# A three-part transformer kernel on one core: first batch in a new written order, second batch's keys on VectorE, third batch's keys behind the last output product, values in parts of 256 and 320 tokens

## The chip, the core and the metric

The kernel runs on one core of a Trainium2 chip. The metric is device time in microseconds of one execution, the median of several runs. Before the change it is 943.38 us (three runs, 940.66 to 943.66).

The engines are TensorE (matrix products, PE in the rows; a transposition is a product with the identity), VectorE (DVE), ScalarE (ACT), GpSimd (POOL) and SyncE (SP), which issues the DMAs. Each takes its instructions in the order in which they are written; semaphores hold them until what they read has been written and what they write over has been read.

## What is computed

Three blocks on 8 batches of 576 tokens: attention against keys and values pooled by 8 (8 heads of 64), a gated MLP with a spatial product, and a mixture of four attention experts. The change touches the first two only.

```python
k_p = k.reshape(B, H, Sp, pool, D).mean(axis=3); v_p = v.reshape(...).mean(axis=3)   # 576 -> 72 keys
attn = softmax(scale * q @ k_p.T)
x = (attn @ v_p) -> [B, S, 512]
h = gelu(x @ w_in)                       # w_in 512 x 1024
u, v = h[..., :512], h[..., 512:]
v_n = (v - mean) / sqrt(var + 1e-6) * g_ln
v_s = w_sg @ v_n + b_sg                  # over the tokens, 576 x 576
x = x + (u * v_s) @ w_out
out = experts(x)                         # q, k, v of 4 experts, causal softmax, top 2 gating
```

## The kernel before

Phase A does attention and the gated MLP batch by batch and stores `x` to DRAM; phase B does the experts for all batches. From the second batch on, most products are made of three float32r matmuls, of high and low halves (`wih`, `wil`, `xh`, `xl`); a `split` copies the high half on ScalarE and subtracts on VectorE. The first batch computes in plain float32, since it has to make these halves of the weights while it runs.

A batch of phase A has these stages. The keys are pooled into the block matrix `kbd` (`pool_k`, L206: per half an addition of 576 columns, one of 288, two of 144). Scores of five chunks of tokens (128, the last 64) go to PSUM (`score`, L274), then maximum, exponential (`probs`, or eight activations per chunk inside `score` for the chunks listed in `AXT`), sum, reciprocal and product `P` (`finish`, L307). `trans` (L324) transposes `P` by five TensorE transpositions and ScalarE copies it to `pth`; from the second batch on VectorE also makes the low half `ptl`. The values are pooled (`pool_v`), and the products with the values give `x` (`av`, in the first batch `av_first`, L373, in two halves of 288 tokens). The projection to `v` comes first (`vfirst`, L445, 32 matmuls in the trace, then `vpart` for the last chunk), then that to `u` (`upart`, L499), each with a gelu on ScalarE. Layer norm (`norm`, `scaled`) is done by VectorE, with the power on GpSimd and the high half on ScalarE. `spatial` (L518) makes four products, each multiplied with `u` by VectorE (L533), copied high by ScalarE (L538) and low by VectorE (L540, the steps `L` in the first batch). `outp` (L546) makes four output products from these; VectorE adds `x` (L560) and takes the low half (L562).

Within a batch, the next batch's scores, finishes and transpositions lie between these products.

The middle batches are written out in `middle`. The first batch's order is a string, `SEQ`: one token is one step (a letter, then its number), and all its instructions on PE, DVE, ACT and POOL keep this order. In it `a`, `b`, `d`, `h`, `g` are loads, `p` pools the first batch's keys, `s`, `x`, `f`, `t` are score, exponential, finish and transposition of a chunk, `y` pools values, `z` is a half of `av_first`. `G` and `W` turn one eighth of `w_in` from 64-bit to 32-bit (`W4` to `W7` are those of `v`, one for each 128 rows; `W0` to `W3` those of `u`), `D` splits it, `Y` is a step of `vfirst`, `V` and `U` the other projections, `n` and `N` the norm, `S` a part of `w_sg`, `o`, `E`, `O`, `Z` the four parts of `w_out`, `P` a spatial product. `K`, `k`, `Q`, `C`, `X`, `F`, `R`, `v` load and pool the second batch's keys (`k`), load `q`, score, exponentiate, finish its chunks, load and pool its values. Tables beside it choose PSUM buffers (`ST`, `TRT`, `AT`, `VT`), the engine that pools keys (`KE`: D for VectorE, P for GpSimd) and the number of dummy transpositions of the identity ahead of a step, which only keep TensorE busy (`idle`, L269: `WS` ahead of a score, `WT` ahead of a transposition, `WV` ahead of a half of `av_first`).

The third batch's keys are pooled by GpSimd, their first half at the start of `middle(1)` (L655); as GpSimd's queue has nothing else then, it starts when the keys have landed.

Of the kernel before, what the change touches and what calls it, by code (L numbers as in the profile page):

```python
# [12 lines left out]
AF = mybir.ActivationFunctionType  # L13
# [3 lines left out]
B, H, S, D = 8, 8, 576, 64  # L17
# [2 lines left out]
NT = 5  # L20
TINY64 = 2.0 ** -30 * 1.265625
NV = ['DD', 'DD', 'DD', 'DD', 'DD']
TRT = ("mm", "tr", "sc", "mm", "mm")
PV = [None, None, 0]
ST = ('mm','mm','sc','tr','mm')
PK = [(0,), (1,), ()]
WOF = 4
XW = 4 * (640 + S)
AXT = {(0, 0), (0, 2), (0, 4), (1, 2), (1, 3), (1, 4)}
FD = {(0,2), (0,3), (0,4), (0, 0), (0, 1), (1, 0), (1, 1), (1, 2), (1, 3), (1, 4)}  # L30
ORD = (mybir.EngineType.PE, mybir.EngineType.DVE, mybir.EngineType.Activation, mybir.EngineType.Pool)
AT = (("tr", "sc"), ("mm", "mm"))
WV = (8,0)
VT = ("sc", "tr")
CT = ("sc", "tr", "sc", "tr", "sc")
XA = (0, 1, 2, 3)
WS = (0, 0, 0, 0, 0)
WT = (14,26,8,0,8)
VE = ('PPP', 'PPP')
KE = ('DD','PP')  # L40
SE = 'DDDD'
SEQ = ("a0 a1 b0 b1 b2 b3 b4 d0 d1 d2 c h2 h3 g h0 h1 p0 p1 s0 x0 s1 x1 s2 x2 f0 s3 x3 s4 t0 f1 x4 t1 "
# [4 lines left out]
TOK = [(i * 128, min(128, S - i * 128)) for i in range(NT)]  # L47


class PhaseA:  # L50


    def __init__(self, ctx, tc, w, ins, x2d):
# [6 lines left out]
        self.EX, self.WO, self.MV = {}, {}, {}  # L60
        self.PT, self.VN, self.QT, self.KV, self.RAW, self.STG = {}, {}, {}, {}, {}, {}


    def load_k(self, b, parts=(0, 1)):
        nc, w = self.nc, self.w
# [307 lines left out]
    def av_first(self, h):  # L373

        nc, mm = self.nc, self.nc.tensor.matmul
        pt, (v, vl) = self.PT[0][0], self.KV[0]
        s = slice(h * HS, h * HS + HS)
        if h == 0:
            xu = self.XU[0] = self.w.tile([128, 2368 * 2], F32, tag="xu", name="xu")
            for p in range(NP):  # L380
                self.X32[0, p] = xu[:, p * S:p * S + S].rearrange("p (a n) -> p a n", a=2)
        x = self.XU[0][:, :NP * S].rearrange("p (c n) -> p c n", c=NP)
        ps = [self.ps.tile([128, 2, 512], F32, tag=t, name="av", bufs=2 if t == "mm" else 1) for t in AT[h]]
        self.idle(ps[0][:, 0, :128], WV[h])
        for p in range(NP):
            r = slice(32 * p, 32 * p + 32)
            mm(ps[p // 2][:, p % 2, :HS], vl[r].rearrange("p a b -> p (a b)"), pt[r, 4, s], start=True, stop=False, skip_group_check=True)
        for p in range(NP):
            mm(ps[p // 2][:, p % 2, :HS], v[:, p], pt[:, p, s], start=False, stop=True, skip_group_check=True)
            if p % 2:  # L390
                nc.scalar.activation(x[:, p - 1:p + 1, s], ps[p // 2][:, :, :HS], AF.Copy)

    def put_x(self, b, p, ps):
        nc, w = self.nc, self.w
# [123 lines left out]
    def spatial(self, b, d):  # L518
        nc, w = self.nc, self.w
        vh, vl = self.VN[b]  # L520
        ps = self.ps.tile([128, 2, 512], F32, tag="mm", name="sp", bufs=2)
        c = slice(d * 128, d * 128 + 128)
        for h in range(2):
            s = slice(h * HS, h * HS + HS)
            o = ps[:, h, :HS]
            for k in range(4):
                nc.tensor.matmul(o, vh[:, k, c], self.ws[0][:, k, s], start=k == 0, stop=False)  # L527
                nc.tensor.matmul(o, vl[:, k, c], self.ws[0][:, k, s], start=False, stop=False)  # L528
                nc.tensor.matmul(o, vh[:, k, c], self.ws[1][:, k, s], start=False, stop=False)  # L529
            nc.tensor.matmul(o, vh[:, 4, c], self.ws[0][:, 4, s], start=False, stop=False)  # L530
            nc.tensor.matmul(o, self.vn2[:, c], self.ws[1][:, 4, s], start=False, stop=True)
        u = self.U.pop((b, d))
        nc.vector.tensor_mul(u, ps[:, :, :HS], u)  # L533
        if d == 0:
            self.GG[b] = w.tile([128, 2368 * 2], F32R, tag="xg", name="g")
        part = lambda i: self.GG[b][:, i * S:i * S + S]
        gh, gl = (part(i).rearrange("p (a n) -> p a n", a=2) for i in (d, 4 + d))
        nc.scalar.activation(gh, u, AF.Copy)  # L538
        self.G[b, d] = (part(d), part(4 + d))
        low = lambda: (nc.gpsimd if b and d < 3 else nc.vector).tensor_sub(gl, u, gh.bitcast(F32))  # L540
        if b:
            low()
        else:
            self.low[d] = low
# [51 lines left out]
    def first(self):  # L596
# [32 lines left out]
        if B > 1:  # L629
            steps.update({  # L630
                "K": lambda i: load_k1(), "k": lambda i: pool_k1(), "Q": lambda i: self.load_q(1), "R": lambda i: load_v1(),
                "v": lambda i: behind(lambda: self.pool_v(1), self.rs), "M": lambda i: self.parts_v(), "C": lambda i: self.score(1, i),
                "X": lambda i: self.probs(1, i),
                "F": lambda i: self.finish(1, i)})
        keep, last = ORD, {}
# [14 lines left out]
    def middle(self, b):  # L650
# [1 line left out]
        n = b + 1  # L652
        more = n < B
        if more:
            self.pool_k(n, PK[0])  # L655
        for t in (0, 2, 4):
            self.vpart(b, t)
            if more and t == 0:
# [478 lines left out]
```

## Time and profile before

| | us |
|---|---|
| median of three runs | 943.38 |
| profiled execution | 941.85 |
| its span, first to last instruction | 940.1 |
| TensorE busy | 913.8 (97%) |
| VectorE busy | 676.8 (72%) |
| ScalarE busy | 513.7 (55%) |
| GpSimd busy | 415.5 (44%) |

The profile's page shows TensorE above 90% in nearly all of its 40 slices; the first two and a few at the start have less. So the stages are read one by one. A row of the timeline gives start, busy time, engine, line, operation, what it writes and reads, and the count; in brackets the idle time just before it and who ended it. Matmuls overlap by their pipeline, so the distance of two starts tells more than the busy time.

### The profile page before, as it was taken

The page shows a single profiled execution, that of the slowest core. Times are in us where ns is not written, and L with a number is a line of the kernel's source. Part 1 is how long each engine was busy: PE and PEld are TensorE (multiplying, and loading weights), DVE is VectorE, ACT ScalarE, POOL GpSimd, SP SyncE. Part 2 cuts the span into 40 slices and gives each one's busy share as a digit, 9 for nine tenths or more (in the row PEclk, how much of TensorE's full clock was granted, in tenths as well). Part 3 has the DMA queues.
Part 4 walks back from the last instruction along what each step waited for, and adds up shares of the span by engine and source line. Part 5 has one row for each costly group of instructions (what it writes and reads, how often), then busy time and mean ns, then how long its engine had stood idle before and what let it go on. Part 6 is the DMA issues. An engine that isn't in the chain of part 4 may idle for free.

```text
span 940.1 us, 18379 instructions
## 1 busy us (share of the span) xinstructions
PE 913.8 (97%) x6496; PEld 858.0 (91%) x6496; DVE 676.8 (72%) x1844; ACT 513.7 (55%) x1280; POOL 415.5 (44%) x590
## 2 busy tenths in 40 slices
PE   6998999999999999999999999899999999999997
PEld 5577999999899899899999999899999999999987
DVE  6899577577586676676675435797978787878785
ACT  4755343343443443434343425677778786777686
POOL 4336268377475683693683440122223232322221
PEclk9999999999999999999999999999999999999999
DMA  9724204214123124024034023435344342525121
GB/s 322 268 68 157 103 12 137 109 42 142 76 85 124 62 74 155 30 74 174 12 116 157 18 97 89 133 86 162 100 138 122 109 141 90 169 64 167 51 63 77
DMA packets 51644, 102.86 MB, mean 109 GB/s; under 512 B 10592, under 2 KB 16736, under 8 KB 50656
## 3 DMA queue, kind: packets, MB, share of 16 engines
q1 hardware_dynamic: 51408, 101.68, 33.2%
q8 instruction: 52, 0.85, 0.4%
q14 instruction: 40, 0.33, 0.1%
q10 hardware_dynamic: 144, 0.00, 0.0%
HBM read 59.72 MB, written 28.31 MB: 94 GB/s over the span
## 4 chain that ended last, share of the span: by engine, by line
PE 79%; DVE 12%; ACT 4%; issue 2%; DMA 1%; SPq 1%; POOL 0%; ACTq 0%; DVEq 0%; POOLq 0%
PE av L1026 4%; PE op L555 4%; PE op L556 4%; PE sc L283 4%; PE op L557 4%; PE up L511 3%; PE sp L529 3%; PE up L513 3%; PE sp L527 3%; PE sp L528 3%; PE up L512 3%; PE vp L442 3%; PE vp L440 3%; PE vp L441 3%; PE t L1006 3%; PE pj L833 3%
## 5 line engine op out<-in xcount | busy, mean ns | idle before, releaser
L980 POOL TENSOR_SCALAR pr<-pr,sm,gw 128x128 f32<-128x128 f32 (+3 forms) x119 | 72.1, 608 | 210.8 <-DVE sm L976 137.5
L964 ACT ACTIVATE pr<-s,sm 128x256 f32<-128x256 f32 (+4 forms) x160 | 83.1, 520 | 41.4 <-DVE sm L961 19.6
L555 PE MATMUL op<-g,woh 128*128 128x288 f32 x256 | 77.8, 308 | 2.0 <-DVE xu L533 1.4
L527 PE MATMUL sp<-wsh,vnh 128*128 128x288 f32 x256 | 78.0, 305 | 0.5 <-DVE xu L533 0.5
L556 PE MATMUL op<-g,woh 128*128 128x288 f32 x256 | 76.7, 300 | 0.8 <-DVE g L540 0.8
L833 PE MATMUL pj<-xbh,wqh 128*128 128x288 f32 x256 | 75.7, 296 | 0.0
L834 PE MATMUL pj<-xbl,wqh 128*128 128x288 f32 x256 | 75.6, 295 | 0.0
L529 PE MATMUL sp<-wsl,vnh 128*128 128x288 f32 x256 | 75.4, 295 | 0.0
L835 PE MATMUL pj<-xbh,wql 128*128 128x288 f32 x256 | 75.4, 295 | 0.0
L528 PE MATMUL sp<-wsh,vnl 128*128 128x288 f32 x256 | 75.4, 294 | 0.0
L557 PE MATMUL op<-g,wol 128*128 128x288 f32 x256 | 75.0, 298 | 0.0
L511 PE MATMUL up<-x,wih 128*128 128x288 f32 x224 | 67.3, 300 | 0.0
L513 PE MATMUL up<-x,wil 128*128 128x288 f32 x224 | 66.2, 295 | 0.0
L512 PE MATMUL up<-x,wih 128*128 128x288 f32 x224 | 65.7, 293 | 0.0
L961 DVE CUSTOM_DVE_ANT_0 s<-s,mk 128x512 f32<-128x512 f32 (+3 forms) x128 | 62.3, 487 | 2.9 <-PE t L1006 2.6
L1011 DVE TENSOR_TENSOR pbl<-t,pbh 128x512 fp32r<-128x512 f32 (+3 forms) x128 | 60.5, 484 | 3.3 <-ACT pbh L1010 1.9
L562 POOL TENSOR_TENSOR x2l<-x2l,x2h 128x576 fp32r<-128x576 f32 x8 | 11.4, 1427 | 111.3 <-ACT x2h L561 111.3
L1006 PE MATMUL t<-ident,pr 128*128 128x128 f32 x320 | 56.4, 278 | 3.3 <-POOL pr L980 3.1
L1026 PE MATMUL av<-pbh,vt 128*128 128x320 f32 (+4 forms) x224 | 56.1, 280 | 2.7 <-ACT pbh L1010 2.7
L283 PE MATMUL sc<-kbd,qt 128*128 128x144 f32 (+1 forms) x320 | 48.0, 297 | 7.7 <-DMA qt<-q_in 7.3
L492 ACT ACTIVATE vnh<-vg,rs 128x512 fp32r<-128x512 f32 (+1 forms) x40 | 27.2, 717 | 51.2 <-POOL rs L474 40.8
L337 ACT ACTIVATE pth<-tr 128x640 fp32r<-128x640 f32 (+3 forms) x40 | 26.0, 653 | 53.1 <-PE tr L336 43.5
(259 smaller groups left out, 3305.7 us busy)
## 6 DMA issues: line engine op xcount, KB each, us to landing
kraw<-k_in SPq DMA_DIRECT2D x16, 576.0 KB, 3.8
x<-x2h SPq DMA_DIRECT2D x32, 288.0 KB, 2.1
x<-x2l SPq DMA_DIRECT2D x32, 288.0 KB, 2.1
xbl<-x SPq DMA_DIRECT2D x32, 288.0 KB, 4.0
xbh<-x SPq DMA_DIRECT2D x32, 288.0 KB, 4.0
kd<-scr SPq DMA_DIRECT2D x64, 144.0 KB, 2.5
out<-o SPq DMA_DIRECT2D x32, 288.0 KB, 3.6
vraw<-v_in SPq DMA_DIRECT2D x16, 512.0 KB, 4.2
```

Of the source, the lines that this page charges most:

```text
L283: nc.tensor.matmul(ps[:m, p // 2, (p % 2) * 144:(p % 2) * 144 + 144], qt[:, p, o:o + m], kbd[:, p, :], start=p % 2 == 0, stop=True, skip_g ...
L511: nc.tensor.matmul(o, self.wi[0][:, kc, c], xh, start=kc == 0, stop=False)
L512: nc.tensor.matmul(o, self.wi[0][:, kc, c], xl, start=False, stop=False)
L513: self.upmm = nc.tensor.matmul(o, self.wi[1][:, kc, c], xh, start=False, stop=kc == 3).ins
L527: nc.tensor.matmul(o, vh[:, k, c], self.ws[0][:, k, s], start=k == 0, stop=False)
L528: nc.tensor.matmul(o, vl[:, k, c], self.ws[0][:, k, s], start=False, stop=False)
L529: nc.tensor.matmul(o, vh[:, k, c], self.ws[1][:, k, s], start=False, stop=False)
L555: nc.tensor.matmul(o, self.wo[0][:, k, c], gh[:, s], start=k == 0, stop=False)
L556: nc.tensor.matmul(o, self.wo[0][:, k, c], gl[:, s], start=False, stop=False)
L557: self.opmm = nc.tensor.matmul(o, self.wo[1][:, k, c], gh[:, s], start=False, stop=k == 3).ins
L833: nc.tensor.matmul(ps, self.wq[0][:, kc, c], xh[:, s], start=kc == 0, stop=False)
L1026: nc.tensor.matmul(ps[:, s - lo:], vt[:, j, 2 * p + e].rearrange("p a d -> p (a d)"), t[:, e, j * PTS + s:j * PTS + up], start=j == 0 and ...
```

## The change

The new order of the first batch is a new string, with new tables of buffers and of dummy transpositions. The second batch's keys go to VectorE (`KE`). In `av_first` the two halves become 256 and 320 tokens (`AZ`). The first half of the third batch's keys waits for the last output product of the first batch (`KL`). A step `v` with another number than 0 could be held back too, but the string has only `v`, which stays as it was. Cut to its core (line numbers below 65 are the same in both; from there the changed kernel's are 13 to 17 higher):

```diff
-TRT = ("mm", "tr", "sc", "mm", "mm")
+TRT = ('mm', 'tr', 'mm', 'mm', 'mm')
-ST = ('mm','mm','sc','tr','mm')
+ST = ('mm', 'tr', 'sc', 'tr', 'mm')
+AZ = ((0, 256), (256, S))
-WV = (8,0)
-VT = ("sc", "tr")
+WV = (0, 6)
+VT = ('tr', 'sc')
-WS = (0, 0, 0, 0, 0)
-WT = (14,26,8,0,8)
+WS = (6, 0, 0, 12, 9)
+WT = (5, 11, 0, 0, 0)
-KE = ('DD','PP')
+KE = ('DD','DD')
+KL = 1
-SEQ = ("a0 a1 b0 b1 b2 b3 b4 d0 d1 d2 c h2 h3 g h0 h1 p0 p1 s0 x0 s1 x1 s2 x2 f0 s3 x3 s4 t0 f1 x4 t1 "
+SEQ = ("a0 a1 b0 b1 b2 b3 b4 d0 d1 d2 c h2 h3 g h0 h1 p0 p1 s0 s1 x0 x1 s2 G5 f0 x2 y0 s3 s4 t0 x4 f1 "
...
+    def behind(self, step, ins, engine):
+        traced = self.nc.cur_bb.bb.instructions
+        n = len(traced)
+        step()
+        for i in traced[n:]:
+            if i.engine == engine:
+                self.tc.add_manual_dep(i, ins.name, mybir.DependencyInfo(mybir.DependencyClass.Sync, mybir.DependencyReason.DATA),
+                                       reason="begun behind it")
+                return
...
-        s = slice(h * HS, h * HS + HS)
+        s = slice(*(AZ[h]))
+        m = s.stop - s.start
...
         if more:
-            self.pool_k(n, PK[0])
+            if b == 1 and KL:
+                self.behind(lambda: self.pool_k(n, PK[0]), self.opmm, mybir.EngineType.Pool)
+            else:
+                self.pool_k(n, PK[0])
```

In the lists that follow `P` is a chunk's probabilities, `tr` and `pth` their transposition in PSUM and in SBUF, `st` the maxima and sums, `sc` scores, `av` the products with the values `v` and `vl`, `w` the 32-bit `w_in` (made from `st` and `g`), `vp` the projection to `v`, `sp` a spatial product, `xu` the array of `x` and `u`, `g` the gated values, `op` an output product.

TensorE, from the second transposition to the projection, before (after its first five transpositions):

```order
L272 MATMUL tr<-ident 128x128 x26
L336 MATMUL tr<-ident,P 128x128 x5
L272 MATMUL tr<-ident 128x128 x8
L336 MATMUL tr<-ident,P 128x128 x5
L272 MATMUL av<-ident 128x128 x8
L387 MATMUL av<-pth,vl_280 128x288 x4
L389 MATMUL av<-pth,v_99 128x288 x4
L336 MATMUL tr<-ident,P 128x128 x5
L272 MATMUL tr<-ident 128x128 x8
L336 MATMUL tr<-ident,P 128x64 x5
L387 MATMUL av<-pth,vl_280 128x288 x4
L389 MATMUL av<-pth,v_99 128x288 x4
```

The same place now:

```order
L285 MATMUL tr<-ident 128x128 x11
L349 MATMUL tr<-ident,P 128x128 x10
L401 MATMUL av<-pth,vl_284 128x256 x4
L403 MATMUL av<-pth,v_99 128x256 x4
L349 MATMUL tr<-ident,P 128x64 x5
L349 MATMUL tr<-ident,P 128x128 x5
L285 MATMUL av<-ident 128x128 x6
L401 MATMUL av<-pth,vl_284 128x320 x4
L403 MATMUL av<-pth,v_99 128x320 x4
```

The dummies (L272, now L285) between the real steps became fewer, the last full chunk and the half one changed places, and the value products have 256 and 320 columns.

VectorE, from the third chunk's `P` of the second batch to the first output product's addition, before:

```order
L316 TENSOR_TENSOR P<-e,st 128x512
L319 TENSOR_TENSOR P<-e,st 128x4x16 x2
L540 TENSOR_TENSOR g<-xu,g 128x576
L312 TENSOR_SCALAR st<-st 64x8
L313 RECIPROCAL st<-st 64x8
L316 TENSOR_TENSOR P<-e,st 64x512
L319 TENSOR_TENSOR P<-e,st 64x4x16 x2
L533 TENSOR_TENSOR xu<-sp,xu 128x576
L340 TENSOR_TENSOR ptl<-tr,pth 128x4x128
L540 TENSOR_TENSOR g<-xu,g 128x576
L341 SCALAR_TENSOR_TENSOR ptl<-pth,cm,tr 128x128
L560 TENSOR_TENSOR op<-op,xu 128x2x288
```

Now, from the low half of the first gated product:

```order
L554 TENSOR_TENSOR g<-xu,g 128x576
L547 TENSOR_TENSOR xu<-sp,xu 128x576
L554 TENSOR_TENSOR g<-xu,g 128x576
L547 TENSOR_TENSOR xu<-sp,xu 128x576
L554 TENSOR_TENSOR g<-xu,g 128x576 x2
L301 TENSOR_REDUCE st<-sc 64x8
L353 TENSOR_TENSOR ptl<-tr,pth 128x4x128
L304 TENSOR_SCALAR st<-st 64x8
L325 TENSOR_SCALAR st<-st 128x8
L354 SCALAR_TENSOR_TENSOR ptl<-pth,cm,tr 128x128
L326 RECIPROCAL st<-st 128x8
```

The multiplications (L533, now L547) and low halves (L540, now L554) stand together ahead of the last three finishes, which come after them with the last score block (L301); the first output product's addition (L574) follows the first of those finishes.

VectorE, from the last splits of `w_in` (`wil`) and `w_sg` (`wsl`) to the first normalisation (`bs`), before:

```order
L155 TENSOR_TENSOR wil<-w_73,wih 128x512
L198 TENSOR_TENSOR wsl<-st_459,wsh 128x576
L155 TENSOR_TENSOR wil<-w_73,wih 128x512
L203 SCALAR_TENSOR_TENSOR wsl<-h_470,cm,st_468 128x576
L155 TENSOR_TENSOR wil<-w_73,wih 128x4x128 x4
L470 BN_STATS bs<-vg 128x6 x2
```

The same place now, up to the first half of the second batch's keys (`kraw`, `kbd`):

```order
L216 SCALAR_TENSOR_TENSOR wsl<-h_436,cm,st_434 128x576
L168 TENSOR_TENSOR wil<-w_73,wih 128x512
L211 TENSOR_TENSOR wsl<-st_443,wsh 128x576
L211 TENSOR_TENSOR wsl<-st_447,wsh 128x576
L224 TENSOR_TENSOR kraw<-kraw 128x576
L225 TENSOR_TENSOR kraw<-kraw 128x288
L228 TENSOR_TENSOR kbd<-kraw 64x2x72 x2
```

The second half of the keys follows with the same three rows, and then `BN_STATS`. Before, these six rows were GpSimd's.

## Rows read from the trace of the kernel before

**Rows 1.** Busy time by stretch: PE, PEld, DVE, ACT, POOL (instructions), granted clock, DMA.

```profile
0.00:105.00 105.00, 92.56 (x514) 73.16 (x515) 85.38 (x162) 58.90 (x167) 42.50 (x66) 0.98 0.54 194
105.00:171.00 66.00, 66.00 (x459) 61.65 (x459) 44.50 (x75) 26.02 (x38) 42.57 (x58) 1.00 0.25 88
```

**Rows 2.** Timeline of TensorE, second transposition to projection; columns as told above.

```profile
18.68 3.03 PE L272 MATMUL tr<-ident 128*128 128x128 f32 x26 [1.22 <-DVE e L296]
...
23.51 1.04 PE L272 MATMUL av<-ident 128*128 128x128 f32 x8
24.56 0.77 PE L387 MATMUL av<-pth,vl 32*128 32x288 f32 x8
...
27.30 0.71 PE L336 MATMUL tr<-ident,P 128*128 128x128 f32 x5
...
32.61 13.90 PE L455 MATMUL vp<-w,xu 128*128 128x512 f32 x32
```

**Rows 3.** Timeline of TensorE, first spatial product.

```profile
69.09 0.39 PE L527 MATMUL sp<-wsh,vnh 128*128 128x288 f32 x1
...
72.89 1.14 PE L283 MATMUL sc<-kbd,qt 128*128 128x144 f32 x8
73.78 0.39 PE L527 MATMUL sp<-wsh,vnh 128*128 128x288 f32 x1
```

**Rows 4.** Timeline of TensorE, begin of the output products and two waits.

```profile
88.11 0.40 PE L555 MATMUL op<-g,woh 128*128 128x288 f32 x1
...
90.09 0.41 PE L556 MATMUL op<-g,woh 128*128 128x288 f32 x1 [0.79 <-DVE g L540]
...
92.05 0.40 PE L555 MATMUL op<-g,woh 128*128 128x288 f32 x1 [1.42 <-DVE xu L533]
```

**Rows 5.** TensorE alone by stretch: length, busy (matmuls), granted clock, DMA share, GB/s.

```profile
93.93:97.34 3.41, 3.41 (x17) 0.50 0.02 5
```

**Rows 6.** Busy time by stretch, output stage of the first and second batch.

```profile
88.10:108.10 20.00, 17.56 (x117) 16.46 (x116) 12.71 (x28) 5.69 (x9) 0.00 (x0) 0.91 0.43 166
159.90:175.20 15.30, 15.30 (x118) 14.82 (x117) 10.13 (x18) 5.39 (x9) 2.74 (x4) 1.00 0.61 225
```

**Rows 7.** Timeline of VectorE, last finishes and first weight steps.

```profile
22.71 0.74 DVE L311 TENSOR_REDUCE st<-e 128x8 f32<-128x576 f32 x1
...
24.81 0.15 DVE L312 TENSOR_SCALAR st<-st 64x8 f32<-64x8 f32 x1
...
25.84 0.35 DVE L319 TENSOR_TENSOR P<-e,st 64x64 f32<-64x64 f32 x2
...
29.80 0.69 DVE L151 SCALAR_TENSOR_TENSOR w<-st,g 128x512 uint32<-128x512 uint32 x1
...
30.87 0.69 DVE L151 SCALAR_TENSOR_TENSOR w<-st,g 128x512 uint32<-128x512 uint32 x1
...
34.21 1.78 DVE L151 SCALAR_TENSOR_TENSOR w<-st,g 128x512 uint32<-128x512 uint32 x1
```

**Rows 8.** Timeline of ScalarE, copy of a transposed chunk.

```profile
28.05 0.70 ACT L337 ACTIVATE pth<-tr 128x640 f32<-128x640 f32 x1
```

**Rows 9.** Timeline of VectorE and GpSimd, keys of first and second batch.

```profile
6.70 0.76 DVE L211 TENSOR_TENSOR kraw<-kraw 128x576 f32<-128x576 f32 x1
...
7.99 0.62 DVE L215 TENSOR_TENSOR kbd<-kraw 64x144 f32<-64x144 f32 x2
...
33.86 1.57 POOL L211 TENSOR_TENSOR kraw<-kraw 128x576 f32<-128x576 f32 x1
...
41.27 1.46 POOL L215 TENSOR_TENSOR kbd<-kraw 64x144 f32<-64x144 f32 x2
```

**Rows 10.** Timeline of VectorE and GpSimd, last norm, first multiplication, third batch's keys.

```profile
61.85 0.75 DVE L496 SCALAR_TENSOR_TENSOR vnh<-vg,rs,vnh 64x512 fp32r<-64x512 f32 x1
...
77.71 0.74 DVE L533 TENSOR_TENSOR xu<-sp,xu 128x576 f32<-128x576 f32 x1
...
85.11 1.39 POOL L215 TENSOR_TENSOR kbd<-kraw 64x144 f32<-64x144 f32 x2
```

More of the change, by code (lines that the diff above doesn't have):

```diff
@@ L31 @@
 ORD = (mybir.EngineType.PE, mybir.EngineType.DVE, mybir.EngineType.Activation, mybir.EngineType.Pool)
-AT = (("tr", "sc"), ("mm", "mm"))
-WV = (8,0)
-VT = ("sc", "tr")
-CT = ("sc", "tr", "sc", "tr", "sc")
+AZ = ((0, 256), (256, S))
+AT = (('tr', 'sc'), ('mm', 'mm'))
+WV = (0, 6)
+VT = ('tr', 'sc')
+CT = ('sc', 'tr', 'sc', 'tr', 'sc')
 XA = (0, 1, 2, 3)
-WS = (0, 0, 0, 0, 0)
-WT = (14,26,8,0,8)
+WS = (6, 0, 0, 12, 9)
+WT = (5, 11, 0, 0, 0)
 VE = ('PPP', 'PPP')
-KE = ('DD','PP')
+KE = ('DD','DD')
 SE = 'DDDD'
-SEQ = ("a0 a1 b0 b1 b2 b3 b4 d0 d1 d2 c h2 h3 g h0 h1 p0 p1 s0 x0 s1 x1 s2 x2 f0 s3 x3 s4 t0 f1 x4 t1 "
[4 rows of a table removed]
+KL = 1
+SEQ = ("a0 a1 b0 b1 b2 b3 b4 d0 d1 d2 c h2 h3 g h0 h1 p0 p1 s0 s1 x0 x1 s2 G5 f0 x2 y0 s3 s4 t0 x4 f1 "
[4 rows of a table added]
 TOK = [(i * 128, min(128, S - i * 128)) for i in range(NT)]
@@ L386, in av_first @@
             r = slice(32 * p, 32 * p + 32)
-            mm(ps[p // 2][:, p % 2, :HS], vl[r].rearrange("p a b -> p (a b)"), pt[r, 4, s], start=True, stop=False, skip_group_check=True)
+            mm(ps[p // 2][:, p % 2, :m], vl[r].rearrange("p a b -> p (a b)"), pt[r, 4, s], start=True, stop=False, skip_group_check=True)
         for p in range(NP):
-            mm(ps[p // 2][:, p % 2, :HS], v[:, p], pt[:, p, s], start=False, stop=True, skip_group_check=True)
+            mm(ps[p // 2][:, p % 2, :m], v[:, p], pt[:, p, s], start=False, stop=True, skip_group_check=True)
             if p % 2:
-                nc.scalar.activation(x[:, p - 1:p + 1, s], ps[p // 2][:, :, :HS], AF.Copy)
+                nc.scalar.activation(x[:, p - 1:p + 1, s], ps[p // 2][:, :, :m], AF.Copy)
     def put_x(self, b, p, ps):
@@ L532, in spatial @@
         u = self.U.pop((b, d))
-        nc.vector.tensor_mul(u, ps[:, :, :HS], u)
+        self.gmul = nc.vector.tensor_mul(u, ps[:, :, :HS], u).ins
         if d == 0:
@@ L631, in first @@
                 "K": lambda i: load_k1(), "k": lambda i: pool_k1(), "Q": lambda i: self.load_q(1), "R": lambda i: load_v1(),
-                "v": lambda i: behind(lambda: self.pool_v(1), self.rs), "M": lambda i: self.parts_v(), "C": lambda i: self.score(1, i),
+                "v": lambda i: self.behind(lambda: self.pool_v(1), self.gmul, mybir.EngineType.Pool) if i else behind(lambda: self.pool_v(1), self.rs), "M": lambda i: self.parts_v(), "C": lambda i: self.score(1, i),
                 "X": lambda i: self.probs(1, i),
```

8 rows, old and new, of the table SEQ are left out of this document.

## The prediction

> **What bounds the kernel now.** I read the busy time by stretch first. From 105 us on TensorE has next to no gap: it is busy 66.00 of 66.00 us in a middle batch, while it is busy only 92.56 of the first 105 us [rows 1]. The change rewrites the order of the first batch and little else, so whatever it brings must come out of those 105 us. Next I read TensorE's timeline there. It falls into three parts.
>
> First, up to 32.61 us, a chain of latencies: scores, softmax, transpositions, products with the values; then the projection starts, 32 matmuls in 13.90 us without a gap [rows 2]. Second, from 32.61 to the first output product at 88.11 [rows 4], TensorE has nearly always work; its first spatial product starts at 69.09 [rows 3]. Third, the output products, from 88.11 to 108.1, where the next batch's value products begin [rows 4, 6]. Here TensorE waits 0.79 us for a low half of the gated values and 1.42 us for a spatial product's multiplication, both VectorE's [rows 4]. [...] The same products of the second batch take 15.30 us with TensorE busy throughout; in the first batch the stretch takes 20.00, with TensorE busy for 17.56 at a mean clock of 0.91 [rows 6]. So about 4.7 us are lost in this one stage, and VectorE, which is late, is the reason. That is the main thing the change can win.
>
> **Up to the projection.** Before, 26 and three times 8 dummy transpositions (8 cost 1.04 us) stand between the real work [rows 2]. Now 11 stand ahead of the second transposition and 6 ahead of the value products' second part; the others went to the scores (12 and 9), where TensorE had to wait anyway, or are gone. I follow the new order with durations of the rows. VectorE has the third chunk of probabilities ready at 22.71, where it turns to the next finish [rows 7]; nothing before this is moved on VectorE. Its transposition (0.6 us, from the five at 27.30, which show 0.71 and overlap what follows) ends at 23.4. The value products of 288 tokens took from 24.56 to 27.30, that is 2.74 us [rows 2]; for 256 tokens they take 2.74 x 256/288 = 2.4, and end near 25.9.
>
> The fourth chunk is now last: its exponential stands behind the third chunk's copy on ScalarE, so it ends at 24.7 (two ScalarE steps after 23.4, each 0.70 by the copy at 28.05, less some overlap [rows 8]). The two last finishes took 3.48 us together before, 22.71 to 26.19, and the one with a sum, up to 24.81, is the longer with 2.1 [rows 7]. So this chunk is ready at 26.85, transposed at 27.45, copied at 28.1. The second part of the products, now 320 tokens, takes 2.74 x 320/288 = 3.0, and ends at 31.2. The weights must be there too: the first column block that the projection reads is now the fourth to be made, at 1.1 us each (from the row at 29.80 to that at 30.87 [rows 7]), so it is there at 26.85 + 4.4 = 31.25. Projection at 31.3 instead of 32.61: **1.3 us gained**. If the late exponential or the weights slip by one step more, nothing is gained; if the copies run closer, 2. So 0 to 2. The first part could have begun a chunk earlier, but it stands behind the third transposition in TensorE's queue; that reserve isn't used.
>
> **Keys on VectorE.** The second batch's keys cost GpSimd from 33.86 to 42.73, 8.9 us; on VectorE one half of the first batch's keys took from 6.70 to 8.61, 1.9 us, so 3.8 for both [rows 9]. They now stand in VectorE's queue behind six of the weight splits and ahead of both first normalisations, so those wait for them. Against that, VectorE's own operations were stretched while GpSimd pooled: a weight step of 0.69 us took 1.78 at 34.21 [rows 7]. I count the two as equal, and with nothing on TensorE's path: before, the last operand of the spatial products was ready at 62.60, 6.5 us ahead of 69.09 [rows 3, 10]. That cover would be gone only if VectorE were 5 us later against a projection that is 1.3 earlier. The scores that need these keys stand behind the projection (31.3 + 13.9 = 45.2) and two gate projections; VectorE has the keys by 26.85 + 8 weight steps at 1.1 + 10 subtractions of that size at 0.7 + 3.8 = 46.5, so they don't wait.
>
> **Projection to the first output product.** TensorE's work is the same, only with the last value tile after the first gate projection. Before, it took 36.5 us to the first spatial product [rows 2, 3], with no wait; I keep that: 67.8. From there, four spatial products at 3.80 (69.09 to 72.89), two score blocks at 0.9, and one transposition of 0.6 make 17.6 [rows 3]; before it took 88.11 - 69.09 = 19.0. The missing 1.4 us are waits for VectorE, whose first spatial multiplication came only at 77.71, five microseconds after its product was done at 72.89 [rows 3, 10]. In the new order that multiplication comes ahead of the softmax finishes, and the finishes of the last three chunks come after all four multiplications, so VectorE has 4 x 0.7 (multiplications), 4 x 0.7 (low halves), two finishes at 2.1 and one score block of 0.9 to do in 17.6 us: 11 (0.7 by the row at 77.71, and the same for others of its size). The value pooling on GpSimd still runs beside it, some 3 us earlier than before, and may stretch it to 14. **1.4 us gained**, bounds 0.5 to 1.4. Output products start at 67.8 + 17.6 = 85.4.
>
> **Output products.** The finishes do not vanish; three go into this stage, with the last score block and its eight exponentials on ScalarE. VectorE is busy for 10.13 us in a middle batch's 15.30 [rows 6]; three finishes without a sum (3.48 - 2.1 = 1.4 each) and a score block of 0.9 make it 15.2. So VectorE is just full. The last spatial product ends at 83.8; multiplication, ScalarE's copy and low half at 0.7 each bring VectorE to 85.9. Then its queue has the score block (0.7), the first chunk's low half (0.9), three finishes (4.2), an addition and a low half of the output (0.7 each) and the second chunk's low half (0.9): 8.1, so it is done at 94.0. The third transposition needs the buffer that this frees, and is due on TensorE at 93.5, after two output products and the begin of a third: 0.5 to 0.6 us of wait. At the end the last chunk's transposition stands behind the first value product, and its copy may cost another 0.3. 15.3 + 0.9 = 16.2 against 20.0: **3.8 us gained**, of it 1.7 through the clock that stays up (3.4 us at half). If VectorE lags 2 us more, and the clock falls after all, all of it goes: bounds 0 to 4.7.
>
> **Third batch's keys.** Their first half ran on GpSimd up to 86.50, over VectorE's late stretch [rows 10]; now it begins behind the last output product, near 101, and takes 4.4 (half of 8.9 [rows 9]). Behind it on GpSimd stand the last low half of the output, the four copies of the next input and the next normalisation's power, for which the spatial products wait; ahead of that one lies the next batch's own projection, as long as the first batch's 13.90 us or longer, and 4.4 us more of work fit in there. On SyncE a value load waits for this buffer, and two stores stand behind it; nobody waits for those until the next output stage. Cost 0; if that cover failed, 1 to 2 us.
>
> **Sum.** 1.3 + 1.4 + 3.8 = 6.5 us off. The profiled execution took 941.85 (span 940.1), which gives 935.4. The runs' median, 943.38, is 1.5 above it and would give 936.9. I take 936.2, between the two.
>
> **Rivals.**
> *The clock falls in the first part.* There are fewer dummy transpositions, and by the new order TensorE waits 1.3 us ahead of the second chunk and 0.7 ahead of the third, close together; before, waits of 0.79 and 1.42 us close together were followed by the fall [rows 4, 5], while one of 1.22 at 18.68 was not [rows 2]. A fall costs up to 1.7 us there, of which about 1 reaches the projection: 937.2; with a second one, 938.5. Chance 0.25.
> [...]
> *VectorE becomes the bound of the output stage.* The three finishes moved there push each copy of a transposition back, TensorE waits three times instead of once, and the clock falls again; the stage takes 20 as before, and only 2.7 us remain: 940.5 or more. For it: VectorE has 15.2 us of work in 15.3. Against it: its work is spread, and only buffers of the transpositions hang on it. Chance 0.12.
> *Slower: the clock stays low in the first part.* If the fall comes in the wait ahead of the second chunk and the short work that follows never brings it back, all TensorE work from there to 31.3 runs at half speed: four transpositions at 0.6, six dummies at 0.8, products of 2.4 and 3.0, 8.6 us, and the projection's beginning 1.7. The projection starts at 39.9 instead of 31.3, and 10.3 - 6.5 = 3.8 us are lost: 947. It decides once the low stretch takes over about two thirds of this part (6.5 of 10.3). Against it: before, the clock rose in a part that was as broken. Chance 0.05.
> *The keys on VectorE do not come for free.* If the splits are as slow without GpSimd beside them, VectorE is 4 to 5 us later, and the spatial products stay just covered; half of the second gain goes: 937.5, inside the forecast's range. Chance 0.08.
>
> **How the numbers follow.** The forecast itself has 0.50: 934 to 938. Low end: all gains at their upper bounds, 2 + 1.4 + 4.7 = 8.1, off 941.85 gives 933.7, and a fall of the clock elsewhere in the run that need not recur is worth 1.7 at most; so 932.0. High end: the second rival, 940.9. I leave out the slower rival and the worst of the second. Faster by over 0.3% (2.8 us, about what a measurement of this kernel can tell from no change) means below 940.5: the forecast, the first and the last rival and a part of the second, 0.84. Within 0.3%: 0.10. Slower: 0.06.
>
> **What would show it.** In the new profile the projection should start at 31 to 31.6, the first output product at 85 to 86, and the next batch's value products near 101, against 32.61, 88.11 and 108.1; no stretch at clock 0.50 between 80 and 105; VectorE's first spatial multiplication within 1 us of its product's end; one or two waits of TensorE under 1 us on a transposition in the output stage. From there on every mark should be shifted by the same 6 to 7 us. I am wrong if the clock is at 0.50 ahead of 32 us, if TensorE waits ahead of the first spatial product, or if the output stage takes over 18 us.

## The result, and the profile after

The changed kernel takes 933.73 us (four runs, 932.62 to 934.83), the kernel before 942.02 in the comparison (940.30 to 943.66): a ratio of 0.9912, 95% interval 0.9886 to 0.9938, 8.3 us less. Forecast was 936.2, range 932.0 to 940.9. A second comparison (experiment 12) gave 932.28 against 943.32, ratio 0.9883 (0.9862 to 0.9904). The profiled execution took 934.04, its span 932.3 (before 940.1).

Busy time by stretch in the changed kernel (length; busy us of PE, PEld, DVE, ACT, POOL with instructions; granted clock; DMA). The first two stretches answer to [rows 1], the last two to [rows 6]:

```profile
0.00:97.00 97.00, 88.41 (x501) 69.99 (x502) 82.78 (x170) 58.62 (x167) 30.70 (x54) 1.00 0.59 204
97.00:163.00 66.00, 66.00 (x459) 61.62 (x458) 44.57 (x76) 26.06 (x38) 45.73 (x62) 1.00 0.30 97
84.90:99.90 15.00, 15.00 (x120) 14.83 (x118) 12.83 (x33) 6.82 (x23) 0.30 (x1) 1.00 0.52 198
151.80:167.10 15.30, 15.30 (x118) 14.84 (x117) 10.14 (x18) 5.37 (x9) 2.73 (x4) 1.00 0.61 226
```

The first batch's output stage is now as dense as the second's: TensorE is busy all of it, at clock 1.00, where it had been busy 17.56 of 20.00 us at 0.91. From 31.4 to 170 us the list of TensorE's waits is empty.

TensorE's timeline, the waits ahead of the projection [rows 2] and then the starts of the first spatial product, the first output product and the next value products [rows 3, 4]:

```profile
21.30 0.77 PE L349 MATMUL tr<-ident,P 128*128 128x128 f32 x5 [0.90 <-DVE P L329]
22.71 0.74 PE L349 MATMUL tr<-ident,P 128*128 128x128 f32 x5 [0.64 <-ACT pth L350]
26.86 0.74 PE L349 MATMUL tr<-ident,P 128*128 128x128 f32 x5 [0.39 <-ACT xu L405]
31.40 3.17 PE L469 MATMUL vp<-w,xu 128*128 128x512 f32 x7
...
67.28 0.39 PE L541 MATMUL sp<-wsh,vnh 128*128 128x288 f32 x1
...
84.91 0.38 PE L569 MATMUL op<-g,woh 128*128 128x288 f32 x1
...
99.35 0.30 PE L378 MATMUL av<-pth,vhi 128*128 128x288 f32 x1
```

VectorE's timeline: second half of the second batch's keys, first and last spatial multiplication, and the step that frees the buffer for the third transposition [rows 9, 10]:

```profile
46.43 0.62 DVE L228 TENSOR_TENSOR kbd<-kraw 64x144 f32<-64x144 f32 x2
...
71.30 0.74 DVE L547 TENSOR_TENSOR xu<-sp,xu 128x576 f32<-128x576 f32 x1
...
83.37 0.76 DVE L547 TENSOR_TENSOR xu<-sp,xu 128x576 f32<-128x576 f32 x1 [2.10 <-PE sp L545]
...
92.45 0.34 DVE L354 SCALAR_TENSOR_TENSOR ptl<-pth,cm,tr 128x128 fp32r<-128x128 f32 x1
```

The first multiplication starts 4.0 us after its product began, against 8.6 before; ahead of the last one VectorE idles 2.1 us. It is no longer late.

Where the time went, by TensorE's starts (us):

| stretch | before | changed | gain |
|---|---|---|---|
| start to projection | 32.61 | 31.40 | 1.2 |
| projection to first spatial product | 36.49 | 35.88 | 0.6 |
| first spatial to first output product | 19.02 | 17.63 | 1.4 |
| from there to the second batch's first product to `u` (126.46, 118.36) | 38.35 | 33.45 | 4.9 |

That is 8.1 us at this mark, and 8.07 to 8.11 at each spatial product up to the end of phase A. Phase B, whose program is the same, adds and takes some: before, the clock falls once more near 592 us (0.50 for 3.41 us from 592.27 on, which costs 1.4 us); then the changed kernel waits 0.8 and 1.0 us for loads of `x` near 722 and 769, the one before 0.7. The spans differ by 7.8.

### The profile page after: what moved, and what is told of

Read it like the earlier page. It is cut to its first block, busy times and chain, and to the rows that moved or that the text cites. A ratio compares the mean times of both kernels' runs of the same rounds, so it can differ in the third digit from the quotient of the medians.

```text
span 932.3 us, 18346 instructions
## 1 busy us (share of the span) xinstructions
PE 909.0 (98%) x6481; PEld 853.5 (92%) x6481; DVE 675.4 (72%) x1852; ACT 513.3 (55%) x1280; POOL 406.6 (44%) x582
## 4 chain that ended last, share of the span: by engine, by line
PE 83%; DVE 8%; ACT 4%; issue 2%; DMA 2%; SPq 1%; POOL 0%; ACTq 0%; DVEq 0%; POOLq 0%
PE sc L296 4%; PE op L569 4%; PE av L1043 4%; PE sp L543 4%; PE sp L541 4%; PE sp L542 4%; PE op L570 4%; PE op L571 4%; PE up L525 3%; PE up L527 3%; PE up L526 3%; PE vp L456 3%; PE vp L454 3%; PE vp L455 3%; PE pj L852 3%; PE pj L850 3%
## 5 line engine op out<-in xcount | busy, mean ns | idle before, releaser
L1027 ACT ACTIVATE pbh<-t 128x512 fp32r<-128x512 f32 (+3 forms) x128 | 51.6, 441 | 3.4 <-PE t L1023 2.5
L552 ACT ACTIVATE g<-xu 128x576 fp32r<-128x576 f32 x32 | 22.0, 687 | 54.4 <-DVE xu L547 54.4
```

## The experiments

The length of a stretch repeats to 0.1 us from kernel to kernel where nothing in it is changed; whole times scatter by 2 us and more, by phase B and by falls of the clock. So the experiments are read from stretches of one profile each: the projection's start (vp; it also moves with the first score, which the loads let begin at 6.85 to 7.72), and above all the time from the first spatial product to the second batch's first product to `u` (tail). A profile is one execution; how often the clock fell in the others is read from the mean granted clock of each run.

| kernel | vp | vp to spatial | spatial to output | tail | median us |
|---|---|---|---|---|---|
| before | 32.61 | 36.49 | 19.02 | 57.37 | 942.02 |
| changed | 31.40 | 35.88 | 17.63 | 51.08 | 933.73 |
| 1 old tail | 32.37 | 35.87 | 17.79 | 53.08 | 936.56 |
| 2 keys on GpSimd | 31.15 | 36.60 | 17.65 | 51.09 | 937.06 |
| 3 third keys early | 31.46 | 35.87 | 17.65 | 51.09 | 935.26 |
| 4 no dummies | 33.79 | 35.87 | 17.65 | 51.09 | 933.82 |
| 5 old tail, third keys early | 32.36 | 35.87 | 18.75 | 56.31 | 940.54 |
| 6 before, third keys late | 32.94 | 36.49 | 17.98 | 55.54 | 940.06 |
| 7 before, new tail | 33.33 | 36.48 | 17.65 | 52.63 | 933.97 |
| 8 before, waits filled | 32.30 | 36.50 | 18.97 | 56.41 | 939.40 |
| 9 finishes early | 31.64 | 35.88 | 17.68 | 53.42 | 935.81 |
| 10 halves | 32.16 | 35.98 | 17.64 | 51.09 | 934.50 |
| 11 as 2, filled | 31.31 | 36.61 | 17.65 | 51.10 | 935.37 |
| 12 changed again | 30.96 | 35.87 | 17.63 | 51.08 | 932.28 |

**1. The old order at the end.** Only `Z3`, the last part of `w_out`, stands behind `X1` here, and ahead of `X0` in the kernel before.

```diff
-... U3 X0 Z3 C2 P0 F0 X1 C3 P1 F1 L1 P2 L0 P3 L2 L3 C4 F2 v F3 F4
+... U3 X0 X1 Z3 C2 F0 P0 C3 F1 L0 P1 C4 F2 L1 P2 F3 L2 F4 P3 L3 v
```

> The changed kernel, only with the end of the first batch's order as it was before: the finishes of the second batch's chunks again between and ahead of the spatial multiplications and low halves. Theory (the order of VectorE's work at the end of the batch makes the gain): the projection stays at 31.4 us, the first spatial product at 67.3, the first output product comes 1 to 2 us later than 84.9, TensorE waits again 0.8 and 1.4 us for VectorE in the first output product, and the granted clock falls to 0.50 behind them; 938.7 to 940.7 us. Rival (the gain comes from the keys that left GpSimd, so that VectorE is no longer stretched, and the order is worth little): the output stage stays under 16 us, no fall of the clock, 933.5 to 935.

The tail became 53.08, only 2.0 us longer; the projection is 1.0 later, for a cause ahead of the edit (the first score is at 7.52 instead of 7.06). One wait came back, and the clock stayed at 1.00 in the profile; of the nine runs only two have a mean clock of 0.999 or more, four have 0.996 or less. Waits of TensorE from 10 to 110 us, the one in the output stage:

```profile
PE op L569 <- DVE xu L547: 1.4, 1, 1.4
```

Both theories miss: the order counts, but alone it doesn't bring back the 57.37 of before.

**2. The second batch's keys back on GpSimd.** `KE = ('DD','PP')`

> The changed kernel, only with the second batch's keys pooled by GpSimd again. Theory (VectorE has slack there, the keys are off the path on either engine): weight steps of VectorE beside the pooling take 1.8 us again instead of 0.7, the last operand of the norm stays ahead of 67.3, all marks of TensorE within 0.3 us; 933.4 to 934.3 us. Rival (keys on GpSimd push its later work, the values' pooling above all, into VectorE's multiplications): the first spatial multiplication stays at 71.3 but the output stage gets waits; 935 to 938 us.

The tail is unchanged, against the rival. But the projection takes 14.47 instead of 13.73 us; 0.46 of the difference is a wait, the rest slower steps of TensorE next to it. TensorE, the last column block of the projection; VectorE, three subtractions beside GpSimd's pooling (0.69 each in the changed kernel):

```profile
42.08 3.70 PE L469 MATMUL vp<-w,xu 128*128 128x512 f32 x8 [0.46 <-DVE w L164]
```

```profile
36.67 3.99 DVE L168 TENSOR_TENSOR wil<-w,wih 128x512 fp32r<-128x512 f32 x3
```

VectorE's last weight step for `v` comes late, and the projection waits for it. So the keys on VectorE are worth 0.7 us in the new order, not nothing. (The median holds more than that: the profile has a fall of the clock near 585 us, shown with experiment 11.) Beside the pooling the subtractions take 1.33 us each, against 0.69.

**3. The third batch's keys early.** `KL = 0`

> The changed kernel, only with the third batch's keys not held back: GpSimd pools their first half near 81 to 85 us, beside VectorE's last multiplications and finishes. Theory (VectorE idles 2.1 us for the last spatial product and TensorE waits for nothing in the output stage): a stretch of up to 3 us in VectorE's steps is mostly taken up, 933.5 to 934.5 us. Rival (VectorE is full in the output stage, 15.2 us of work in 15.1): TensorE waits again for low halves and transpositions, output stage over 16.5 us, possibly with a fall of the clock; 936 to 939 us.

All marks within 0.1 us of the changed kernel's, though one low half of VectorE took 2.03 instead of 0.74 us beside GpSimd. With the new order the slack takes it up; the held-back keys gain nothing there. The median, 935.26, lies above the theory's range all the same: in the profile the clock is at 0.50 from 583.2 to 590.1, in phase B, whose program is the same.

**4. No dummy transpositions.** `WS`, `WT`, `WV` all zero.

> The changed kernel, only without any dummy transposition (49 left out). Theory A (they bring the clock up and keep it up): the granted clock rises later than 11.3 us, or falls between 12 and 31 us; the projection starts at 32.5 to 35 us, 935 to 938 us. Theory B (they only fill waits, real work keeps the clock): the clock is 1.0 from about 11.3 us on, the projection starts at 31.0 to 31.4, 933.3 to 934 us.

TensorE reaches the second transposition 4 us too early and stands still. Timeline of TensorE, then stretches of it (length, busy, clock, DMA):

```profile
21.43 0.97 PE L349 MATMUL tr<-ident,P 128*128 128x128 f32 x5 [4.14 <-DVE P L329]
```

```profile
17.30:21.40 4.10, 0.00 (x0) 1.00 1.01 276
21.40:28.80 7.40, 7.04 (x27) 0.54 1.06 388
28.80:33.80 5.00, 4.21 (x28) 1.00 1.02 412
```

Theory A: the real work behind the wait runs at half clock, and the projection starts 2.4 us later (1.8 of it from the first score on: 26.12 against 24.34). All six runs have a mean clock of 0.996 or less. Phase B gave the time back: from the last batch's first spatial product to the end, this profile is 3.3 us shorter than the changed kernel's, 1.8 of it because it has none of the waits for loads near 722 and 769; the rest isn't explained. So the whole time, 933.82, doesn't show the loss. The 11.3 us of the expectation show in the scores: in the changed kernel the median of their matmuls is 448 ns from 9 to 11.1 us and 286 from 11.35 on, while the view of the granted clock has 1.00 there throughout.

**5. Old order and early third keys together.** Edits 1 and 3.

> The changed kernel with two parts undone together: the old order at the end of the first batch, and the third batch's keys not held back. Measure: the time from the first spatial product to the second batch's first product to u; before 57.37 us, changed kernel 51.08, with the old order alone 53.07, with the early keys alone 51.09. Theory (with the old order VectorE is late, and then GpSimd's pooling of the third batch's keys beside it makes it later; with the new order there is slack for it): 55.5 to 57.4 us, waits of 0.8 and 1.4 us in the first output product, perhaps a granted clock of 0.50 behind them. Rival (the two costs add up singly, 2.0 and 0.0): 53.0 to 53.4 us, no fall of the clock.

The tail of before nearly returns. Waits of TensorE from 60 to 125 us, and the clock behind them:

```profile
PE op L569 <- DVE xu L547: 2.2, 2, 1.4
PE op L570 <- DVE g L554: 0.8, 1, 0.8
```

```profile
90.70:94.20 3.50, 3.28 (x14) 0.51 0.39 166
```

So the two don't add up singly (2.0 and 0.0): together they cost 5.2 us, some 1.7 of it by the clock, half of 3.4 us.

**6. The kernel before, third batch's keys late.** The same hold as in the change, alone.

> The kernel before, only with the first half of the third batch's keys held back behind the last output product of the first batch. Measure: from the first spatial product to the second batch's first product to u, 57.37 us before. Theory (GpSimd's pooling from 82 to 86.5 us makes VectorE, late by its order, later still): the last multiplication of a spatial product comes 1 to 2 us earlier against the first spatial product than before (22.2 us), 54 to 56 us. Rival (VectorE is late by its order and the values' pooling alone, the third batch's keys have no part in it): 57.0 to 57.4 us.

The last multiplication starts 20.36 instead of 22.16 us after the first spatial product, and the tail is 1.8 shorter, with the fall of the clock still there (0.51 from 92.0 to 95.4). The pooling from 82.22 to 86.5 [rows 10] was a part of VectorE's lateness. The theory holds.

**7. The kernel before, new order at the end.**

> The kernel before, only with the new order at the end of the first batch, from the exponentials of the second batch's first chunk on. Measure: from the first spatial product to the second batch's first product to u, 57.37 us before, 51.08 changed. Theory (the order alone gives VectorE the slack that takes up what GpSimd stretches): 51.0 to 52.0 us, no wait over 0.5 us in the output stage, granted clock 1.0 there, 936 to 938 us. Rival (the order is worth only the 2.0 us that undoing it cost in the changed kernel): 55.0 to 55.6 us, 940 to 941 us.

No wait, and the two stretches from the first spatial product to the next value products are those of the changed kernel, 17.65 and 14.44. The tail is still 1.5 longer, because the clock fell behind them. TensorE by stretch:

```profile
88.00:102.00 14.00, 14.00 (x110) 1.00 0.66 241
102.00:105.50 3.50, 3.50 (x29) 1.00 0.32 121
105.50:109.00 3.50, 3.50 (x17) 0.51 0.22 87
```

It fell without any pause ahead. The other three runs have a mean clock of 1.000 and take 933.66 to 934.21 us. The order at the end alone makes the stage what it is, and with it most of the whole gain: these three runs still have the old front, whose 1.8 us up to the first spatial product show as about 1 us against the changed kernel's eight runs (median 932.75).

**8. The kernel before, dummies in the two waits.**

```diff
+                if first and k == 3:
+                    self.idle(ps[:, 1, 288:416], 11)
                 nc.tensor.matmul(o, self.wo[0][:, k, c], gh[:, s], ...)
+                if first and k == 2:
+                    self.idle(ps[:, 1, 288:416], 7)
                 nc.tensor.matmul(o, self.wo[0][:, k, c], gl[:, s], ...)
```

> The kernel before, only with 7 and 11 dummy transpositions in the first output product, ahead of the two matmuls that wait 0.79 and 1.42 us for VectorE: TensorE is busy there, and VectorE is as late as before. Measure: from the first spatial product to the second batch's first product to u, 57.37 us before. Theory (the pauses bring the clock down): granted clock 1.0 from 88 to 108 us, 55.5 to 55.9 us (1.7 less, half of the 3.41 us at clock 0.50). Rival (the clock falls there for another reason): 0.50 for 3.4 us again, 57.2 to 57.6 us.

No fall in the stage:

```profile
87.70:106.90 19.20, 17.79 (x135) 1.00 0.46 177
```

But the waits were shortened, not filled. Waits of TensorE from 85 to 108 us:

```profile
PE op L558 <- ACT g L538: 0.9, 1, 0.9
PE op L558 <- DVE xu L533: 0.7, 1, 0.7
PE op L561 <- DVE g L540: 0.4, 1, 0.4
```

The 0.7 lies ahead of the first output product; 0.9 and 0.4 come close together behind the dummies, and the clock stayed up even so. The tail is 0.95 shorter, not 1.7: with the dummies the first product's matmuls stand in their written order, so less real work falls into the waits, and the one of 0.4 us for the last low half is new. The time is 939.40, 3.3 us less (ratio 0.9967, 0.9954 to 0.9980), although VectorE is as late as before. Eight of its ten runs have a mean clock of 1.000; of the 50 runs of the kernel before in these comparisons, two. So these eight have no fall near 590 us either, where nothing was edited.

**9. The finishes early, the multiplications still first.**

```diff
-... P0 F0 X1 C3 P1 F1 L1 P2 L0 P3 L2 L3 C4 F2 v F3 F4
+... P0 F0 X1 C3 P1 F1 L1 P2 F2 L0 C4 P3 F3 L2 F4 L3 v
```

> The changed kernel, only with the finishes of the second batch's last three chunks and the last score block back among the spatial multiplications, each behind the multiplication of its product and ahead of the next, as P2 F2 L0 C4 P3 F3 L2 F4 L3; the first multiplications stay ahead of the first finishes. Measure: from the first spatial product to the second batch's first product to u, 51.08 us changed, 53.07 with the whole old order, no fall of the clock in either. Theory (three finishes are 4.2 us of VectorE ahead of the last low halves, and only 2.1 us of idle time stand against them): the last low half is 2 to 3 us later than 84.9 us, TensorE waits 1 to 1.5 us in the first output product, 52.3 to 53.1 us. Rival (VectorE was late because the first multiplication came 8 us behind its product's begin, and the late finishes are no part of it): no wait of TensorE, 51.0 to 51.3 us.

The tail is 53.42, 2.3 longer, as bad as the whole old order. TensorE's waits from 60 to 125 us:

```profile
PE op L570 <- DVE g L554: 1.1, 2, 0.7
PE tr L349 <- DVE ptl L354: 0.3, 1, 0.3
```

The theory holds, though the last low half comes 4.9 us later (89.77), not 2 to 3, and the tail lies 0.3 above its range: what counts is that the last finishes come behind the low halves. The waits explain 1.4 of the 2.3 us; the rest isn't seen.

**10. Halves of 288.** `AZ = ((0, HS), (HS, S))`

> The changed kernel, only with the values in two halves of 288 tokens instead of 256 and 320. Measure: from the first score (7.06 us) to the projection (31.40), 24.34 us; 24.1 to 24.9 in the other kernels with this front. Theory (the second half is made longer, so its end decides, and the weights are there only at 31.24 anyway): within 0.3 us of that, 24.1 to 24.7 us, as 0.3 us less in the second half meets a second half that can't begin before the last chunk is transposed. Rival (the first 256 tokens need only the first two chunks, and begin earlier): with 288 tokens the first half waits for a third chunk, 25 to 25.5 us.

From the first score to the projection 24.68, inside the scatter. But the rival's wait is there:

```profile
24.50 0.77 PE L401 MATMUL av<-pth,vl 32*128 32x288 f32 x8 [0.89 <-ACT pth L350]
```

From the third transposition to the projection it is 9.28 (22.88 to 32.16) against 8.69 us (22.71 to 31.40), and 8.69 again in experiments 1, 2 and 3. So 256 and 320 are worth 0.6 us: the rival's mechanism at about its lower bound.

**11. Experiment 2 with phase B's waits filled.**

```diff
+            if b == 0 and p == 0 and u in (2, 3, 4):
+                for _ in range((8, 6, 5)[u - 2]):
+                    nc.tensor.transpose(ps[:, 0], self.ident, self.ident)
```

> The kernel of the second experiment (changed kernel, second batch's keys on GpSimd; all its runs had a mean granted clock of 0.996 or 0.998), with 8, 6 and 5 dummy transpositions in the begin of phase B, ahead of the three transpositions of the first batch that wait 1.04, 0.72 and 0.95 us for GpSimd near 581 to 585 us. Theory (these pauses bring the clock down, in some alignments): granted clock 1.0 through 575 to 600 us and in nearly every run, 934 to 935.5 us instead of 937.06. Rival (the falls near 585 come from something else, such as the DMA load there): mean clock 0.998 or less in most runs, 936.5 to 937.5 us.

In the profile the clock is 1.00 through the place. TensorE from 575 to 600 us, here:

```profile
575.00:600.00 25.00, 23.76 (x178) 1.00 0.54 147
```

and in experiment 2:

```profile
575.00:600.00 25.00, 21.85 (x151) 0.93 0.52 146
```

935.37 lies in the theory's range, but only two of six runs have a mean clock of 1.000 (none of six in experiment 2), so falls elsewhere remain, and the intervals against the kernel before (0.9896 to 0.9935, and 0.9920 to 0.9958) overlap. Inconclusive as to the size.

**12. The changed kernel again.** No edit.

> The changed kernel once more, for the spread of its clock and time on the same chip as the others. Theory (its gain of 8.3 us has some 5 us from the order and some 3 us from falls of the clock that do not occur): mean granted clock 1.0 in most runs, 933 to 935 us. Rival (that none of the four runs had a fall was chance): runs with 0.998 and 0.996 as often as in the experiment with the third batch's keys early, which stands at the same marks, and a median of 934.5 to 936 us.

932.03 to 932.88, mean clock 0.999 or 1.000 in all four, as in the first four (1.000). No version tried is faster than this.

## Why the prediction was right, point by point

**Up to the projection: right.** 1.3 forecast, 1.2 found, and by the terms that were added up: the last chunk's probabilities were ready at 26.98 (26.85 forecast), the second part of the value products took 3.01 us (3.0), the fourth weight block was there at 31.24 (31.25). But 0.2 of the 1.2 came with the first score (7.06 against 7.28), which the loads set. The rest isn't one profile's luck: from the first score to the projection it is 24.89 to 25.82 us in the four kernels with the old front (means 25.4), 23.59 to 24.86 in the eight with the new one (24.2). The rival of a falling clock did not come true: 1.00 over waits of 0.90, 0.64 and 0.39. In experiment 4 it fell, behind a wait of 4.14 (0.54 from 21.40 to 28.80). The slower rival, a clock that never comes back, has no sign: even there it was back at 28.8. What it was weighed against, that the clock rose before in a part as broken, shows in the scores' matmuls of the kernel before (median 447 ns from 9 to 11.9 us, 286 from 12.1 on), not in the view of the granted clock, which has 1.00 there throughout.

**Keys on VectorE: the term was mis-sized.** I counted 0; in the new order they are worth 0.7 (experiments 2 and 11: 36.60 and 36.61 against 35.87). I looked for the cover at the last operand of the spatial products, and left out that the projection's last column block waits for VectorE's last weight step for `v`, which in the new order comes in time without GpSimd beside it and 0.46 us late with it (experiment 2). The keys were ready at 47.05, against 46.5 forecast. The rival for these keys has a price that does not follow: half of 1.4 us on 936.2 is 936.9, not 937.5.

**Projection to the first spatial product: 0.6 not forecast.** I kept 36.5, it was 35.88. The product counts are equal, and the kernel before has no entry in its list of waits there, though the same 36.49 stands in all four profiles with its front. TensorE's starts show where it lies. In the kernel before, the step from one matmul to the next is 0.47 us at 53.75, ahead of one that ScalarE's gelu of the last value tile released, and 0.45 at 67.68, ahead of a score that a product to `u` released, where 0.24 is usual. It is 0.52 at 45.91, where 0.43 is usual, and a score takes 0.08 longer. The changed kernel has none of these, and together they are the 0.6. Which move in the order removes them, no run separates.

**First spatial to first output product: right in size, half right in reason.** 17.6 forecast, 17.63 found. I put the 1.4 us on the order alone, and in the old kernel the order alone does bring them (17.65, experiment 7). But holding the third batch's keys gives 1.0 of it in the old order (19.02 to 17.98), and taking back the order in the new kernel costs only 0.2 (17.79).

**Output stage: the step that failed, on the safe side.** 3.8 forecast, 4.9 found, above the upper bound of 4.7. I let the third transposition wait 0.5 to 0.6 us for a buffer that VectorE frees at 94.0. It was due at 93.23, and VectorE was done at 92.8: the stage began 0.5 earlier, and three finishes cost about 1.2 us each, not 1.4 (87.22 to 88.40, 89.07 to 90.24 between other steps). Nor did the last chunk cost 0.3. So the stage took 15.1 us, not 16.2. (The next value products start 14.44 us behind the first output product, 20.03 before; but the last chunk's transposition, which stood ahead of them, now comes behind the first of them, so the gain is taken at the product to `u`.) VectorE as the bound, with 12.83 us busy in 15.0, did not happen; experiment 9 shows how near it is, with three finishes placed a little earlier.

**Third batch's keys: right in the new order, and more in the old.** Cost and gain 0 (experiment 3), but 1.8 us in the kernel before (experiment 6). Two causes of one lateness: the order alone takes all of it away (experiment 7), the keys alone a part, and what one is worth depends on whether the other is still there.

**The clock: the mechanism right in part, the size too small.** I gave it 1.7 us at one place, half of the 3.41 us at 0.50 [rows 5]; in the kernel before a matmul of an output product starts every 0.24 us there and every 0.13 once the clock is back at 1.00. Runs of the kernel before have a mean clock of 0.996 or less in 40 of 50 cases (median 943.2), 0.998 in eight (940.7), 1.000 in two (939.0). The changed kernel has 0.999 or more in all eight (932.75). Without a fall on either side the gain is thus about 6 us (939.0 to 932.75, the first from two runs only), and the marks say the same: 8.1 less 1.7, half of the fall's 3.4 us. The rest of the gain, 2 to 5 us by the comparison, is falls that don't occur, among them those near 592 us in phase B, whose program is the same.

The first rival rests on pauses that lie close together, 0.79 and 1.42 us with a fall behind them [rows 4, 5]. The traces agree in part. With the pauses shortened the clock stayed up (experiment 8, 1.00 from 87.70 to 106.90), and it fell behind one of 4.14 us (experiment 4); but pauses of 0.9 and 0.4 us remained in experiment 8, behind one of 1.4 us the clock stayed up in the profile of experiment 1 and behind one of 1.4 it fell in that of experiment 6, and a fall came without a pause in experiment 7. That a pause alone decides is not shown.

**The range.** The time lies in it near the low end, for I took all gains' upper bounds to be unlikely together; of two of them one was reached (1.4 us) and one passed (4.7). The middle part, 934 to 938, which had the chance of 0.50, is missed by 0.3 us, and by 1.7 in experiment 12. Of the signs named, the projection's start, VectorE's first multiplication (0.2 us behind its product's end at 71.07) and the clock between 80 and 105 us came as said. The first output product (84.91) and the value products (99.35) came earlier than 85 and 101, no transposition of the output stage waits, and the later marks are shifted by 8.1 us, not 6 to 7. The second rival's price mixes two bases: with 2.7 us left it is 939.2 off the profiled execution or 940.7 off the median, so the high end of the range, 940.9, goes by about the median, the low end by the profile.

## What to carry to other kernels

When an engine that is off the bound is late at the end of a stage, ask for each of its steps who waits for it in the next 5 us: here the last three softmax finishes, of which TensorE read the first 13.8 us after it was ready (86.72 and 100.54 in the kernel before), stood ahead of three low halves that it needed at once. Taking back the new place alone costs 2 us, with a second engine working beside it 5, of it 1.7 by the clock. Undo each of two suspected causes alone and both together, since slack hides either. And when a few tenths of a per cent matter, compare marks inside the trace, and the granted clock of each run, before the medians.

## What was not expected of the hardware

The granted clock falls to 0.50, for 3.4 us or (experiments 3, 4 and 6) for about 6.8, in some executions and not in others at the same place with nearly the same waits: near 580 to 592 us the kernel before and the changed kernel both have waits of 1.04, 0.72 and 0.66 us (the third 0.95 in experiment 2), and it fell in the kernel before and in experiments 2, 3 and 6, but stayed in the changed kernel and in experiments 1, 4, 5, 7, 8, 9, 10 and 12. What decides it, the runs here do not show. In experiment 7 it fell while TensorE had been busy without a gap for over 17 us; what stood right ahead were 16 products of only 32 rows among others of 128, as they do in every kernel here. And 49 dummy transpositions, which lie in waits, save about 2 us at the projection.
